# Rebuilding the first periods of a fused attention and feed-forward kernel, and the order of its row minima

## The chip, the cores and the metric

The kernel runs on one core of one Trainium2 chip. The metric is device time in microseconds (us) from launch to the end; lower is better. The engines are TensorE (PE in the profile; its weight loads are PEld), VectorE (DVE), ScalarE (ACT), GpSimd (POOL) and SyncE (SP, which only issues transfers here).

## The reference

Attention with a threshold, followed by a two-layer feed-forward network (called MoE in the names). Shapes: q, k, v are 8 batches x 8 heads x 576 rows x 64; w_in is 512 x 2048, w_out is 2048 x 512; the output is 4608 x 512, all in float32.

```python
scores = scale * np.matmul(q, k.transpose(0, 1, 3, 2))
thresh = np.max(scores, axis=-1, keepdims=True) - tau        # tau = 0.02
scores = np.where(scores >= thresh, scores, -1000000000.0)
scores = scores - np.max(scores, axis=-1, keepdims=True)
attn = np.exp(scores)
attn = attn / (np.sum(attn, axis=-1, keepdims=True) + 1e-09)
x = np.matmul(attn, v)                  # heads side by side: 4608 tokens x 512
h = x @ w_in
g = np.maximum(0.01 * h, h)
out = g @ w_out
```

## The kernel before

**Periods.** The work is cut into 72 periods, nine for each batch: eight periods of 256 query rows of one pair of heads (block 0, pairs 0 to 3; block 1, pairs 0 to 3), and one for the last 64 rows ("tails") of all eight heads. Each turn n of the loop at line 463 emits, in one order written out by hand, the instructions of period n on every engine together with work of other periods. Every engine executes its own instructions strictly in this order, so an instruction that waits holds up all that are behind it on its engine.

In period n:
- PE computes the scores (line 227): four tiles of 128 x 576, for two row blocks c and two heads h, into one PSUM buffer `sc` of five banks. One bank is shared by a piece of head 0 (called a12) and a piece of head 1 (b12). The piece that comes second waits for a signal: an empty instruction (line 246) on POOL, that waits for the last matmul of the first piece. It stands behind POOL's earlier work.
- DVE copies each tile to SBUF with its row minimum (line 257, function `copies`, four instructions), makes the thresholds (`th`, line 259, one small instruction for each period: its start is used below as the mark of a period), then the masked weights of three tiles (line 282, `weights`), and the reciprocals of the row sums (`rec`, line 288, `finish`).
- ACT computes the exponentials: three plain ones (line 271, `exp_plain`), and for the fourth tile a steep Prelu and an exponential with a row sum (lines 276 and 277, `exp_steep`). `rec` needs that row sum.
- In turn n+1 POOL spreads `rec` into the weight tile (line 292, `widen`), and SP issues a transposing transfer wT<-w (line 297, `turn_w`).
- Two turns after its scores (PV_LAG = 2), PE multiplies the transposed weights by v (line 309, `pv`), and DVE scales the result into the token group x (line 329, `evacuate`).
- A group of 256 tokens is complete after four periods. Its layer 1 (line 349, eight units) and layer 2 (line 362, sixteen units) are then queued, and each turn takes two units of layer 1 and four of layer 2 off the queues. This is exactly the rate at which groups arrive. ACT applies the leaky function (line 351) and copies the output (line 368).

**Operands.** q and k of float32 are split into two float16 parts, high and low. On POOL a unit (one pair of heads of q or k) takes three instructions: scale (line 144), cast (150) and subtract (154). The units of the very start are split by ACT (high, line 164) and DVE (low, line 165) in `split_now`. `turn` transposes a unit on PE (line 183) and copies it from PSUM on ACT or DVE (line 190, tails line 186); the k tails are copied once more within SBUF by POOL (line 188). From batch 1 on, units are split and turned ahead of their batch; ten units for each batch, so one or two in a period, none in some.

**Buffers that couple the engines.** The PSUM tag "h" has two buffers; transposes, layer 1 and pv go through them in turn, so the next one waits until ACT or DVE has read the last but one. The score copies and exponentials have one buffer for each tile.

**Start.** q and k of batch 0 are loaded pair by pair, with the k tails on SP behind the first k pair; POOL issues the four w_in loads ahead of the loop (they change float32 to float16 on the way), and the w_out loads in turns 3 to 6. v of batch 0 is cast by POOL in turns 2 and 3.

Of the kernel before, what the change touches and what calls it, by code (L numbers as in the profile page):

```python
# [36 lines left out]
def kernel(  # L37
# [44 lines left out]
    def load_tails(b, which):  # L82
        t = sb.tile([128, 2, 2, 64], FP32, tag="rawt", bufs=2, name="rawt")
        src = SRC[which][b, :, MAIN:S, :].rearrange("(u sh) p d -> u p sh d", u=2)
        for u in range(2):
            nc.sync.dma_start(out=t[ds(64 * u, 64), :, :, :].rearrange("p s h d -> p (s h) d"), in_=src[u])
        tails[b, which] = t
# [35 lines left out]
    turned, halves, scaled = {}, {}, {}  # L123
# [44 lines left out]
    def turn(key, copy=None):  # L168
        copy = copy or nc.scalar.copy
        b, p, which = key  # L170
        dst, half = turned_of(b, which), halves.pop(key)
        n = 2 if p == "t" else 4
        c0 = 0 if which == "q" else 64
        if p == "t":
            c0 = MAIN if which == "q" else 0
# [3 lines left out]
        for x in range(2):  # L179
            for t in range(n):  # L180
                for h in range(2):
                    o = tp[ds(64 * h, 64), x, :, t, :] if p == "t" else tp[ds(64 * h, 64), x, t, :]
                    nc.tensor.transpose(o, half[:, x, t, h, :], ident[:, :])  # L183
        if p == "t":
            for x in range(2):
# [3 lines left out]
        else:  # L189
            copy(out=dst[:, :, p, ds(c0, 512)], in_=tp[:, :, :, :].rearrange("d x t p -> d x (t p)"))  # L190
# [38 lines left out]

    def scores(st):  # L230

        (a00, a01), (b01, b00) = pieces(0, 0), pieces(0, 1)
        (a11, a12), (b12, b11) = pieces(1, 0), pieces(1, 1)
        todo = [[(1, a12), (0, a00), (0, a01), (1, a11)], [(0, b00), (0, b01), (1, b11), (1, b12)]]
        todo = [[(c, x, i) for c, x in row for i in range(3)] for row in todo]
        at_, signal = [0, 0], None
        while todo[0] or todo[1]:
# [3 lines left out]
            for mm in product(st, c, h, x, i):  # L241
                if (h, x) == (1, b12) and i == 0:
                    tc.add_manual_dep(mm.ins, signal.ins.name, BEHIND, reason="the row halves share a bank")
                last = mm
            if (h, x) == (0, a12) and i == 2:
                signal = nc.gpsimd.nop()
                tc.add_manual_dep(signal.ins, last.ins.name, BEHIND, reason="the row halves share a bank")

    TILES = ((0, 1), (0, 0), (1, 0), (1, 1))

    def copies(st):
        st.mn = sb.tile([128, 4], FP32, tag="mn", bufs=2, name="mn")
        st.th = sb.tile([128, 4], FP32, tag="th", bufs=2, name="th")
        st.s = {}
        for n, t in enumerate(TILES):
            st.s[t] = sb.tile([128, 576], FP32, tag=f"s{n}", bufs=1, name="s")
            nc.vector.tensor_scalar(out=st.s[t][:, :], in0=sc[:, ds(PLACE[t], 576)], scalar1=-1.0 / UNIT, scalar2=None,  # L257
                                    op0=AX.mult, op1=AX.min, accum_out=st.mn[:, n : n + 1])
# [3 lines left out]
        st.e = {}  # L262
# [23 lines left out]
    def finish(st):  # L286
# [27 lines left out]
    def evacuate(st, n):  # L314
# [17 lines left out]
        if done:  # L332
            nu = 8 if xg.tokens == 256 else 4
            l1q.extend((xg, u, nu, n + 1) for u in range(nu))
# [62 lines left out]
    def split_at(n, key):  # L397
        if key[0]:
            at(pool_at, n - 2, lambda key=key: split_scale(key))
            at(pool_at, n - 2, lambda key=key: split_high(key))  # L400
            at(low_at, n - 1, lambda key=key: split_low(key))
        else:
            at(pool_at, n - 1, lambda key=key: split_pool(key))
        at(turns_at, n, lambda key=key: turn(key))

    for b in range(1, B):
        base = PERB * (b - 1)
        for i, (s, w_) in enumerate(((0, "k"), (0, "q"), (1, "k"), (1, "q"))):
            at(loads_at, base + ((-2, -1, 2, 3)[i] if b > 1 else (1, 1, 3, 3)[i]),
               lambda b=b, s=s, w_=w_: load_main(b, s, w_))  # L410
        for i, w_ in enumerate("kq"):
# [127 lines left out]
```

## Time and profile before

| | us |
|---|---|
| median of 3 runs | 527.36 (525.57 to 527.87) |
| the profiled execution | 526.85 |
| its span, first to last instruction | 525.1 |
| th of period 0 | 18.87 |
| th of periods 1, 2, 3, 4 | 25.84, 33.41, 43.93, 50.50 |
| th of periods 5, 6, 7, 8, 9 | 57.07, 64.71, 72.22, 82.25, 89.20 |
| th of periods 63 and 71 (the last) | 437.90, 486.15 |

"th" is the start of the threshold instruction of a period in the timeline of the profiled execution. The 1.75 us between the span and the profiled execution's time lie outside the recorded instructions. Busy shares over the span are PE 90%, DVE 83%, ACT 80% and POOL 49%; they mix a start in which engines wait, a middle in which three of them are nearly full, and a last part of layer 1 and layer 2 alone.

### The profile page before, as it was taken

The page shows a single profiled execution, that of the slowest core. Times are in us where ns is not written, and L with a number is a line of the kernel's source. Part 1 is how long each engine was busy: PE and PEld are TensorE (multiplying, and loading weights), DVE is VectorE, ACT ScalarE, POOL GpSimd, SP SyncE. Part 2 cuts the span into 40 slices and gives each one's busy share as a digit, 9 for nine tenths or more (in the row PEclk, how much of TensorE's full clock was granted, in tenths as well). Part 3 has the DMA queues.
Part 4 walks back from the last instruction along what each step waited for, and adds up shares of the span by engine and source line. Part 5 has one row for each costly group of instructions (what it writes and reads, how often), then busy time and mean ns, then how long its engine had stood idle before and what let it go on. Part 6 is the DMA issues. An engine that isn't in the chain of part 4 may idle for free. (4 is left out here: it accounts for less than half of the span.)

```text
span 525.1 us, 18850 instructions
## 1 busy us (share of the span) xinstructions
PE 472.8 (90%) x7744; PEld 372.1 (71%) x7744; DVE 435.1 (83%) x1231; ACT 422.3 (80%) x714; POOL 256.3 (49%) x410
## 2 busy tenths in 40 slices
PE   4666768998989999999999999999999999999995
PEld 3444556776777777777777777777777777777783
DVE  1778868999899999999899989999899989999300
ACT  3567678888989998898989998898989998778541
POOL 5889953655375645654384636563385531100000
PEclk9999689999999999999999999999999999999999
DMA  8978999588988699978998699789988796666511
GB/s 204 241 178 175 201 199 209 112 171 195 205 179 183 123 225 227 173 146 203 215 171 176 170 207 215 160 130 225 201 155 202 158 192 144 122 102 151 133 42 61
DMA packets 230806, 90.34 MB, mean 172 GB/s; under 512 B 201024, under 2 KB 227648, under 8 KB 230720
## 3 DMA queue, kind: packets, MB, share of 16 engines
q1 hardware_dynamic: 227488, 84.43, 76.7%
q0 software_dynamic: 2688, 4.19, 4.7%
q8 instruction: 60, 0.98, 0.8%
q10 hardware_dynamic: 544, 0.52, 0.3%
q14 instruction: 26, 0.21, 0.1%
HBM read 36.70 MB, written 9.44 MB: 88 GB/s over the span
## 5 line engine op out<-in xcount | busy, mean ns | idle before, releaser
L257 DVE TENSOR_SCALAR_CACHE_REDUCE s<-sc 128x576 f32<-128x576 f32 x288 | 199.0, 748 | 12.0 <-PE sc L227 11.5
L282 DVE SCALAR_TENSOR_TENSOR w<-s,th,e 128x576 f16<-128x576 f32 x216 | 184.2, 876 | 8.6 <-ACT e L271 1.1
L271 ACT ACTIVATE e<-s,mn 128x576 f16<-128x576 f32 x216 | 158.7, 773 | 20.2 <-DVE s L257 19.2
L362 PE MATMUL o<-wout,g 128*64 128x512 f16 x1152 | 148.9, 380 | 5.0 <-ACT osb L368 3.5
L349 PEld LDWEIGHTS <-win 128*64 128x64 f16 x2560 | 127.4, 110 | 29.2 <-issue 16.0
L349 PE MATMUL hp<-x,win 128*64 128x256 f16 x2048 | 134.4, 273 | 8.4 <-ACT kT L190 4.5
L227 PE MATMUL sc<-kT,qT 64*128 64x256 f16 (+7 forms) x1920 | 128.4, 298 | 12.0 <-DVE s L257 4.7
L292 POOL CAST w<-rec 128x256 f16<-128x256 f32 x72 | 28.7, 399 | 211.8 <-DVE rec L288 199.6
L227 PEld LDWEIGHTS <-qT 64*128 64x128 f16 (+1 forms) x1920 | 97.9, 101 | 35.0 <-issue 19.5
L351 ACT ACTIVATE g<-hp 128x512 f16<-128x512 f32 x144 | 84.6, 588 | 13.0 <-PE hp L349 13.0
L362 PEld LDWEIGHTS <-g 128*64 128x64 f16 x1152 | 69.6, 110 | 35.5 <-issue 8.5
L154 POOL TENSOR_TENSOR half<-scaled,half 128x512 f16<-128x512 f32 (+1 forms) x77 | 82.5, 1079 | 0.6
L309 PE MATMUL pv<-wT,v 128*64 128x256 f16 (+1 forms) x960 | 55.6, 251 | 12.2 <-DMA wT<-w 6.7
L309 PEld LDWEIGHTS <-v 128*64 128x64 f16 x960 | 44.6, 112 | 25.9 <-POOL v L105 5.3
L277 ACT ACTIVATE w<-s,minus_tau 128x576 f16<-128x576 f32 x72 | 55.8, 775 | 5.8
L276 ACT ACTIVATE s<-s,th 128x576 f32<-128x576 f32 x72 | 55.8, 775 | 0.9 <-DVE th L259 0.9
L183 PE MATMUL tp<-ident,half 128*64 128x128 f16 x1152 | 49.3, 236 | 8.0 <-ACT half L164 5.1
L150 POOL CAST half<-scaled 128x512 f16<-128x512 f32 (+1 forms) x77 | 52.1, 676 | 4.9
L183 PEld LDWEIGHTS <-half 128*64 128x64 f16 x1152 | 38.6, 119 | 22.1 <-issue 15.9
L190 ACT COPY kT<-tp 128x1024 f16<-128x1024 f16 x32 | 32.3, 1010 | 21.4 <-PE tp L183 21.4
L144 POOL TENSOR_SCALAR scaled<-raw 128x512 f32<-128x512 f32 x62 | 40.7, 657 | 10.2 <-DMA raw<-in_q_dram 8.3
L190 ACT COPY qT<-tp 128x1024 f16<-128x1024 f16 x31 | 31.4, 1014 | 14.1 <-PE tp L183 14.0
(32 smaller groups left out, 231.6 us busy)
## 6 DMA issues: line engine op xcount, KB each, us to landing
vraw<-in_v_dram SPq DMA_DIRECT2D x16, 512.0 KB, 5.0
out_dram<-osb SPq DMA_DIRECT2D x16, 512.0 KB, 3.7
raw<-in_k_dram SPq DMA_DIRECT2D x14, 512.0 KB, 4.7
raw<-in_q_dram SPq DMA_DIRECT2D x14, 512.0 KB, 4.4
win<-in_moe_w_in_dram POOLq DMA_DIRECT2D x4, 512.0 KB, 11.5
wout<-in_moe_w_out_dram POOLq DMA_DIRECT2D x4, 512.0 KB, 6.8
wT<-w SPq DMA_TRANSPOSE x72, 5.9
raw<-in_k_dram SPq DMA_DIRECT2D x4, 256.0 KB, 11.0
```

The lines of the kernel that those rows point to most:

```text
L154: nc.gpsimd.tensor_tensor(out=halves[key][:, 1, 0:n, :, :], in0=scaled.pop(key)[:, 0:n, :, :], in1=halves[key][:, 0, 0:n, :, :], op=AX.sub ...
L183: nc.tensor.transpose(o, half[:, x, t, h, :], ident[:, :])
L190: copy(out=dst[:, :, p, ds(c0, 512)], in_=tp[:, :, :, :].rearrange("d x t p -> d x (t p)"))
L227: yield nc.tensor.matmul(out=o, lhsT=lhs, rhs=turned[st.b, "k"][rows, kx, pair, ds(key0, n)], start=(i == 0), stop=(i == 2), skip_group_ch ...
L257: nc.vector.tensor_scalar(out=st.s[t][:, :], in0=sc[:, ds(PLACE[t], 576)], scalar1=-1.0 / UNIT, scalar2=None, op0=AX.mult, op1=AX.min, acc ...
L271: nc.scalar.activation(out=st.e[t][:, :], in_=st.s[t][:, :], func=AF.Exp, bias=st.mn[:, n : n + 1], scale=-1.0)
L276: nc.scalar.activation(out=z, in_=z, func=AF.Prelu, bias=st.th[:, n : n + 1], scale=-1.0, alpha=1e20)
L282: nc.vector.scalar_tensor_tensor(out=w_of(st, t), in0=st.s[t][:, :], scalar=st.th[:, n : n + 1], in1=st.e[t][:, :], op0=AX.is_le, op1=AX.mult,
L309: nc.tensor.matmul(out=o, lhsT=v16[st.b % 2][:, 2 * c + u if st.tail else st.p, blk, :], rhs=rhs, start=(i == 0), stop=(i == 4), skip_grou ...
L349: nc.tensor.matmul(out=hp[ds(64 * c, 64), jj, :], lhsT=w_in16[:, i, ds(128 * j + 64 * c, 64)], rhs=g.x[:, i, :], start=(i == 0), stop=(i = ...
L351: nc.scalar.activation(out=g.g[:, ds(nj * u, nj), :], in_=hp[:, :, :], func=AF.Prelu, bias=0.0, scale=1.0, alpha=0.01)
L362: nc.tensor.matmul(out=g.o[ds(64 * c, 64), :], lhsT=g.g[:, j, ds(128 * m + 64 * c, 64)], rhs=w_out16[:, j, :], start=(j == 0), stop=(j == ...
```

## The change

It does eight things.

1. The two transfers of batch 0's k tails go from SP's queue (behind the first k pair) to ACT's queue (behind the first q pair); k of pair 1 follows at once on SP.
2. The first three units are handled one after the other, each split, transposed and copied before the next: k tails, then k of pair 0, then q of pair 0. The tails are copied by DVE.
3. k and q of pair 1 are split by ACT and DVE (`split_now`), no longer by POOL.
4. The four w_in loads go from ahead of the loop into turns 1 and 2, the w_out loads from turns 3 to 6 into turns 4 to 7. v of batch 0 is cast in turns 1 and 2.
5. The scores are emitted in another order: b12 is now the first piece of head 1 and a12 the last of head 0, so a12 waits for the signal. In periods 0 to 3 the signal is on ACT, later on POOL as before.
6. In every period the row minimum of tile (0, 0) is emitted within the scores, behind the piece that shares its bank, and the matmuls behind it are declared independent of it. `rec` of the period before comes next, then the other three tiles.
7. Where a turn has two units, ACT copies the first, computes the first exponential, and copies the second.
8. In turns 0 to 5, pv and its evacuation stand ahead of MoE and ahead of the weights, and a group that is completed there starts layer 1 in the same turn, that is one turn earlier.

```diff
     def load_tails(b, which, eng=None):
...
-            nc.sync.dma_start(out=t[ds(64 * u, 64), ...], in_=src[u])
+            (eng or nc.sync).dma_start(out=t[ds(64 * u, 64), ...], in_=src[u])
...
-    def turn(key, copy=None):                     # transposes and copies
+    def turn(key):                                # transposes only; keeps tps[key]
+    def take(key, copy=None):                     # the copies out of PSUM
...
+    TILES = ((0, 0), (0, 1), (1, 0), (1, 1))      # was ((0, 1), (0, 0), (1, 0), (1, 1))
     def scores(st):
-        todo = [[(1, a12), (0, a00), (0, a01), (1, a11)], [(0, b00), (0, b01), (1, b11), (1, b12)]]
+        todo = [[(0, a00), (0, a01), (1, a11), (1, a12)], [(1, b12), (1, b11), (0, b01), (0, b00)]]
...
+                if first is not None:
+                    tc.declare_no_dep(mm.ins, first.ins, reason="other banks")
-                if (h, x) == (1, b12) and i == 0:
+                if (h, x) == (0, a12) and i == 0:
                     tc.add_manual_dep(mm.ins, signal.ins.name, BEHIND, reason="the row halves share a bank")
-            if (h, x) == (0, a12) and i == 2:
-                signal = nc.gpsimd.nop()
+            if (h, x) == (1, b12) and i == 2:
+                signal = (nc.scalar if st.n < 4 else nc.gpsimd).nop()
+            if (h, x) == (0, a11) and i == 2:
+                first = copy_min(st, 0)
...
+    def copies(st, before):
+        if before:
+            recip(before)
+        copy_min(st, 1)
+        copy_min(st, 2)
+        copy_min(st, 3)
...
     load_pair(0, "q", nc.scalar)
-    load_tails(0, "k")
+    load_tails(0, "k", nc.scalar)
+    load_pair(1, "k", nc.sync)
     load_pair(1, "q", nc.scalar)
-    load_pair(1, "k", nc.sync)
...
-    for i in range(4):
-        load_w(i)
-        at(pool_at, 3 + i, lambda i=i: load_w(4 + i))
+    first = units(0)
+    for key in (first[2], first[0], first[1]):
+        split_now(key)
+        turn(key)
+        take(key, None if key == first[0] else nc.vector.tensor_copy)
+    for key in first[3:5]:
+        split_now(key)
+    for key in first[5:7]:
+        split_pool(key)
+    for i, key in enumerate(first[3:9]):
+        at(turns_at, i // 2, key)
+    for key in first[7:9]:
+        at(pool_at, 0, lambda key=key: split_pool(key))
+    for i in range(4):
+        at(pool_at, 1 + i // 2, lambda i=i: load_w(i))
+        at(pool_at, 4 + i, lambda i=i: load_w(4 + i))
+    at(pool_at, 1, lambda: cast_vtails(0))
+    for p in range(NP):
+        at(pool_at, 1 + p // 2, lambda p=p: cast_v(0, p))
+    at(pool_at, 2, lambda: split_pool(first[9]))
+    at(turns_at, 3, first[9])
...
     while n < N + PV_LAG or l1q or l2q or stores:
+        early = n < 6
...
-        for f in turns_at.get(n, []):
-            f()
+        keys = turns_at.get(n, [])
+        for key in keys:
+            turn(key)
+        for key in keys[:1]:
+            take(key)
+        if st:
+            exp_plain(st, 0)
+        for key in keys[1:]:
+            take(key)
         for f in pool_at.get(n, []):
             f()
-        if st:
-            exp_plain(st, 0)
+        if early:
+            pv_of(n, n)()
         for half in range(2):
...
-        if n >= PV_LAG and n - PV_LAG < N:
-            pv(periods[n - PV_LAG])
+        x = (lambda: None) if early else pv_of(n, n + 1)
         if st:
             weights(st, 0)
             weights(st, 1)
-        if n >= PV_LAG and n - PV_LAG < N:
-            evacuate(periods[n - PV_LAG], n)
+        x()
         if st:
             weights(st, 2)
-            finish(st)
```

## The prediction

> **What bounds the kernel now.** I read the page first, then the busy times by stretch, the timeline up to period 9, the waits, and the transfers of single stretches. A period is marked by its th (line 259).
>
> ```profile
> span 525.1 us, 18850 instructions
> PE 472.8 (90%) x7744; PEld 372.1 (71%) x7744; DVE 435.1 (83%) x1231; ACT 422.3 (80%) x714; POOL 256.3 (49%) x410
> ```
>
> ```profile
> 18.87:89.20 70.33, 48.99 (x672) 37.40 (x673) 57.11 (x151) 50.70 (x83) 53.00 (x75) 0.90 0.98 197
> 89.20:437.90 348.70, 335.71 (x5747) 266.66 (x5748) 323.43 (x919) 312.01 (x529) 186.91 (x299) 1.00 0.87 179
> 437.90:486.15 48.25, 46.80 (x714) 36.11 (x712) 45.36 (x137) 38.76 (x69) 4.58 (x12) 1.00 0.69 140
> ```
>
> Columns: stretch, length, busy PE, PEld, DVE, ACT, POOL, PE clock, share of the DMA engines, GB/s. The first nine periods take 7.8 us each, the next 54 take 6.46, the last eight 6.03. In the middle PE is busy 96%: there PE leads and DVE follows closely. At the end DVE leads (45.4 of 48.3). In the first stretch no engine is full but the DMA engines are (0.98). From the last th to the end, 39 us, PE works alone at layers 1 and 2; the change leaves that as it is.
>
> So the start holds most of what can be won. DVE needs 57.1 us there plus 0.27 idle for each period (the least in any period), 59.5 together; 10.8 are waits. The timeline shows where:
>
> ```profile
> 15.18 0.82 PE L227 MATMUL sc<-kT,qT 64*128 64x256 f16 x5 [2.31 <-POOLq L246]
> ...
> 18.87 0.60 DVE L259 TENSOR_SCALAR th<-mn 128x4 f32<-128x4 f32 x1
> ...
> 35.28 0.42 PE L309 MATMUL pv<-wT,v 128*64 128x256 f16 x1 [4.35 <-POOL v L105]
> ...
> 38.10 0.42 DVE L329 TENSOR_TENSOR x<-pv,wT 128x256 f16<-128x256 f32 x1 [2.25 <-PE pv L309]
> ...
> 75.51 0.83 PE L309 MATMUL pv<-wT,v 128*64 128x256 f16 x10 [3.36 <-DMA wT<-w]
> ```
>
> Period 0 loses 2.3 us because the signal stands behind POOL's splits; period 3 waits for the casts of v on POOL; period 8 waits for a transposing transfer. Why that one is late, two stretches of the DMA view tell:
>
> ```profile
> q0 software_dynamic: 375, 0.38, 93.0%
> ...
> wT<-w SPq DMA_TRANSPOSE x1, 9.2
> ```
>
> ```profile
> q1 hardware_dynamic: 2855, 0.79, 83.5%
> ...
> wT<-w SPq DMA_TRANSPOSE x1, 5.0
> ```
>
> The first is 48.5 to 51.5 us: only q0, the queue of the weight loads, moves (0.38 MB), none of SP's q1, and the wT issued just before takes 9.2 us. The second is 24 to 29 us without q0: 5.0 us. From 56.5 to 58.5 us q0 moved 0.41 MB and q1 twelve packets. So a weight load of 0.52 MB holds wT up for 2.6 us (at that rate) to 4.1 (at 128 GB/s); the wT of 62.65 took 12.8.
>
> **The change, part by part.** Sums are against the profiled execution, 526.85 us, 0.5 under the median.
>
> *Setup.* k tails now come first, and every unit waits for the one before. The tails are worked on at 6.79 now; in ACT's queue, with no weight loads beside them, I take 5.9 (6.8 at worst). Their two issues, 1.41 on SP now, push ACT's table load (1.28) to 4.5 and q of pair 1 behind them, both ahead of need. From there, by the rows of lines 164, 165, 183, 186, 190: tails split, eight transposes (0.64), two copies: 1.8; k of pair 0: low parts 0.72, transposes 0.6, ACT copy 1.0: 2.4; q likewise 2.5. Scores start at 12.6 instead of 10.38, which costs 2.2. But they no longer meet the signal on POOL: 3.3 us (2.50 + 0.82) bring them to 15.9, the first minimum is done beside them, three of 0.68 and 0.2 follow: th of period 0 at 18.1. **-0.8** (ends -0.8 and +0.1).
>
> *Pair 1 on ACT and DVE* (1.34 and 1.43) lies ahead of 15.2, where DVE needs scores: nothing. If scores came earlier it would cost those 1.4. POOL loses 4.8 us (two units of 2.4).
>
> *Periods 1 and 2.* The signal on ACT stands behind the steep exponentials of the period before; behind the waiting matmul stand the turns and pv on PE. The loop is: signal, five matmuls 0.82, 16 transposes 0.96, take 1.0, exp 0.70, take 1.0, two exps 1.40, steep 1.6: 7.5 us. Now it is 6.96 and 7.58. th comes at 25.6 and 33.1: **-0.3 so far**.
>
> *Period 3.* The loads' issues (0.6 each on POOL) stand ahead of the casts (vtails 0.85, pairs 1.25 each) in turn 1; v's first two pairs are still cast by 28.3, so that wait goes. Next late is wT of period 0: issued at 23.6 with two w_in loads beside it, 23.6 + 5.0 + 2 x 2.6 = 33.8. PE wants it at 32.8. If it is not through when loads 3 and 4 begin (about 33), it lands at 39. I take 34, nearer to the row of 2.6: x at 35.7, three weights 2.6, minima and th: 41.6 instead of 43.93. **-2.3 so far** (a wT at 39: +2.7).
>
> *Period 4.* Two w_in loads (5.2 us) and batch 1's first rows (2.7 us) stand ahead of the next wT: it lands at 44, while PE is ready at 39. x now stands ahead of all three weights, so DVE waits from 41.6 to 45: th at 51.4. **+0.9 so far** (ends -2.5 and +6).
>
> *Periods 5 to 7.* Layer 1 starts in turn 5 behind x, which stands behind th: its Prelu on ACT holds the exponentials behind it. This period costs about 2 us more (first layer-1 period now: 7.64 against 6.57 before it), and the next ones go at 7.1 to 7.6, ACT's sum with two takes. **+1.9 at th of period 7.**
>
> *Periods 8 to 10.* w_out comes one turn later, and layer 1 pauses in turn 9, being a turn ahead. Period 8 then takes 7.6 instead of 10.04, and the pause gives 0.3: **-0.6 in all for the start**. The kernel gains nothing else from the early group, since two units a turn is the rate of arrival.
>
> *From period 10 on.*
>
> ```profile
> DVE rec L288 <- ACT w L277: 11.0, 24, 0.9
> ...
> PE hp L349 <- ACT kT L190: 6.4, 11, 0.7
> ...
> PEld L227 <- POOLq L246: 0.2, 1, 0.2
> ```
>
> (89 to 487 us: waited in total, times, longest.) Putting the first minimum ahead of rec covers DVE's 11.0 us, and 0.13 in every period where rec follows the last weights (39.26 to 39.39): up to 8 us more. But PE has 6.15 us of its own in a period with one turn (scores 1.58, transposes 0.47, layers 3.46, pv 0.64) against DVE's 5.94 to 6.4, so DVE's gain counts only where DVE leads: the last eight periods (0.2 each, 1.6) and about half of the others by 0.05 to 0.1. The second take behind the first exponential ends 1.65 us after the first take, and the second layer-1 unit wants its buffer after 1.73: nothing while the exponential's input is ready, up to 0.7 us in some 12 periods if not. The 6.4 us stay. rec, and so POOL's work, moves back by 0.68. **-3.0** (ends -7 and +4).
>
> Sum: -0.6 - 3.0 = -3.6, that is 523.2 us.
>
> **Rivals.**
>
> *A, more.* The wT transfers are not held up by w_in and the start keeps DVE's pace. For: the DMA engines were idle in 36 to 40 us. Against: 48.5 to 51.5. Starting from 41 at period 3, six periods of 6.7 give th of period 9 at 81, 8 us earlier: 515.8. Chance 0.17. The Trainium skill (DMA: Bandwidth & Descriptors, "Queues, rings and completion order") says that a DMA engine takes turns between the queues it has work for, packet by packet; by that rule the two transfers would advance together and this rival would be nearer. The trace disagrees: twelve packets of q1 against 400 of q0 in 56.5 to 58.5 us.
>
> *B, nothing.* The first minimum still waits for the end of all scores, as it did in period 0 (idle 7.81, though its tile was long done), or PE leads throughout; the middle gives 0: 526.2. Chance 0.20.
>
> *C, slower.* w_in holds up both wT: the first lands at 39, the second at 49, and x ahead of the weights passes both waits of 5 us on to DVE; one of them is half absorbed later. +8.5: 531.7. For: q0 and wT got 115 to 130 GB/s together, and one wT took 12.8 us. Against: two weight loads of 2.6 us fit between turns 1 and 2. It decides when the first wT lands later than 36. Chance 0.16.
>
> *D, slower or even.* POOL's signal. With rec 0.68 later, POOL's splits end later; in the periods where it has 5.3 us of work and 1.1 idle, the signal would stop PE by up to 0.5. Two such periods a batch, 6 us, and the middle's gain gone: 529 (526.2 to 532). Against: the wait is 0.2 us now in the whole middle. Chance 0.08.
>
> **How the numbers follow.** The forecast has 0.39: 523.2, its own range 519 to 527. A difference under 0.5% of the median (2.6 us) cannot be told from none, so faster is below 524.7, slower above 530.0. Faster: 0.30 of the forecast, A, and 0.03 of B: 0.50. Same: 0.09 of the forecast, 0.15 of B, 0.03 of D: 0.27. Slower: C, 0.05 of D, 0.02 of B: 0.23. The range reaches from A to C: 514 to 532.
>
> **What would show it.** Scores of period 0 start near 12.6 with no wait for the signal; th of periods 0, 3, 4, 9 near 18.1, 41.6, 51.4, 88.9; the row of pv waiting for v gone, one of pv or x waiting for wT in turns 2 and 3 in its place; rec no longer waiting for ACT; last eight periods 5.8 each. Wrong: th of period 9 outside 81 to 96, or the middle's 54 periods off 6.46 by over 0.12.

## The result, and the profile after

The changed kernel takes 549.50 us (median of 4 runs, 547.55 to 555.57) against 526.74 us (4 runs) before: a ratio of 1.0452 with a 95% interval of 1.0364 to 1.0540. It is slower by about 23 us, outside the predicted range. Ratios here and below leave out executions over 1.5% longer than the shortest of the same kernel; medians are of all executions. The profiled run took 548.35 us with a span of 546.6, against 526.85 and 525.1 before.

The page of the changed kernel, its first lines:

```profile
span 546.6 us, 18926 instructions
PE 472.4 (86%) x7744; PEld 369.4 (68%) x7744; DVE 447.4 (82%) x1237; ACT 423.4 (77%) x716; POOL 259.1 (47%) x404
```

PE is busy as long as before (472.4 and 472.8 us), so the 21.5 us more in the span are idle time of PE. The busy times by stretch say where (columns as in the prediction; each stretch runs from the same th to the same th as there):

```profile
22.24:111.41 89.17, 48.33 (x678) 37.31 (x678) 56.26 (x152) 51.91 (x84) 47.11 (x71) 0.73 1.02 154
111.41:460.92 349.51, 335.09 (x5734) 264.26 (x5736) 332.61 (x919) 310.96 (x527) 197.37 (x300) 1.00 0.87 181
460.92:507.02 46.10, 46.10 (x719) 35.67 (x716) 44.90 (x137) 39.67 (x70) 4.60 (x12) 1.00 0.73 145
```

The first nine periods take 89.17 instead of 70.33 us, the middle 349.51 instead of 348.70, the last eight periods 46.10 instead of 48.25. With th of period 0 late by 3.4 us (22.24, not 18.87), the start loses 22.2 us, the middle 0.8, the end gains 2.2, and what follows the last th takes 0.6 longer: together 21.5. The granted clock was lower in the start (0.73 against 0.90), but PE's busy time there is not longer (48.33 against 48.99 us), so the clock is not what costs the time.

Within the start one period holds most of it. Period 3, from th to th, first in the kernel before and then in the changed one:

```profile
33.41:43.93 10.52, 6.59 (x52) 4.28 (x53) 6.46 (x17) 4.43 (x9) 10.03 (x18) 1.00 0.57 110
```

```profile
35.62:64.04 28.42, 4.84 (x42) 3.45 (x43) 5.95 (x17) 6.07 (x12) 5.00 (x11) 0.58 1.23 122
```

It lasts 28.42 us, all engines together compute little in it, and the DMA engines are full (1.23; shares of packets that overlap in time add up to over 1). The timeline of the changed kernel names the transfer that all wait for:

```profile
7.46 1.28 ACT L164 ACT_TABLE_LOAD   x1 [7.46 <-DMA rawt<-in_k_dram]
...
16.85 3.06 PE L232 MATMUL sc<-kT,qT 64*128 64x384 f16 x24 [0.79 <-DVE qT L195]
...
22.24 0.67 DVE L275 TENSOR_SCALAR th<-mn 128x4 f32<-128x4 f32 x1
...
27.97 1.32 POOL L114 DMA_DIRECT2D win<-in_moe_w_in_dram  x2
28.06 9.99 SPq L312 DMA_TRANSPOSE wT<-w  x1
...
33.99 1.06 POOL L114 DMA_DIRECT2D win<-in_moe_w_in_dram  x2
...
44.52 18.12 SPq L312 DMA_TRANSPOSE wT<-w  x1
57.28 1.28 PE L324 MATMUL pv<-wT,v 128*64 128x256 f16 x10 [22.11 <-DMA wT<-w]
58.59 0.43 DVE L344 TENSOR_TENSOR x<-pv,wT 128x256 f16<-128x256 f32 x1 [22.43 <-PE pv L324]
61.11 0.62 POOL L144 TENSOR_SCALAR scaled<-raw 128x512 f32<-128x512 f32 x1 [23.04 <-DMA raw<-in_k_dram]
66.36 1.28 PE L324 MATMUL pv<-wT,v 128*64 128x256 f16 x10 [4.25 <-DMA wT<-w]
```

The wT of period 0 is issued at 28.06, beside four loads of w_in, and pv, which needs it, starts at 57.28: 29 us instead of 5. Three engines stop behind it for 22 to 23 us each. PE stands at pv, and the scores of the next period are queued behind pv. DVE stands at x, which in the early group is ahead of the weights. POOL stands at batch 1's raw rows: their issue on SP comes behind the transposing transfer, which held SP for 9.99 us (the next one for 18.12), and once issued, at 38.10, the first of them takes 22.9 us to land (4.2 in the kernel before). The DMA view of the changed kernel from 39 to 54 us shows the two queues at work:

```profile
DMA packets 1029, 1.04 MB, mean 70 GB/s; under 512 B 787, under 2 KB 833, under 8 KB 1029
...
q1 hardware_dynamic: 813, 0.24, 66.1%
q0 software_dynamic: 216, 0.80, 49.6%
```

A share of 100% is 16 engines over these 15 us. A packet of q1 (mostly wT) therefore took on average 0.661 x 16 x 15 / 813 = 195 ns and one of q0 (the weights) 551 ns, and both queues together moved 70 GB/s. Where wT runs without the loads, q1's packets take 23 ns (shown with the experiments).

The waits from th of period 9 to the last th:

```profile
POOL w L307 <- DVE rec L303: 176.0, 58, 5.3
...
PE hp L364 <- ACT kT L195: 7.3, 12, 0.7
```

The row of rec waiting for ACT (11.0 us before) is gone; the row of PE's layer 1 waiting for kT stays, as predicted.

### The profile page after: what moved, and what is told of

Read it like the earlier page. It is cut to its first block, busy times and chain, and to the rows that moved or that the text cites. A ratio compares the mean times of both kernels' runs of the same rounds, so it can differ in the third digit from the quotient of the medians.

```text
span 546.6 us, 18926 instructions
## 1 busy us (share of the span) xinstructions
PE 472.4 (86%) x7744; PEld 369.4 (68%) x7744; DVE 447.4 (82%) x1237; ACT 423.4 (77%) x716; POOL 259.1 (47%) x404
## 4 chain that ended last, share of the span: by engine, by line
PE 57%; ACT 7%; DVE 2%; issue 1%; DMA 1%; POOL 0%; POOLq 0%; DVEq 0%
PE o L377 18%; PE hp L364 16%; PE sc L232 14%; PE pv L324 5%; PE tp L180 4%; ACT kT L195 3%; ACT e L286 1%; DMA wT<-w 1%; ACT osb L383 1%; ACT qT L195 1%; ACT g L366 1%; DVE s L265 1%; DVE w L297 0%; DVE th L275 0%; DVE x L344 0%
## 5 line engine op out<-in xcount | busy, mean ns | idle before, releaser
L265 DVE TENSOR_SCALAR_CACHE_REDUCE s<-sc 128x576 f32<-128x576 f32 x288 | 204.1, 746 | 4.8 <-PE sc L232 1.7
L297 DVE SCALAR_TENSOR_TENSOR w<-s,th,e 128x576 f16<-128x576 f32 x216 | 191.6, 907 | 11.5 <-ACT e L286 4.1
L286 ACT ACTIVATE e<-s,mn 128x576 f16<-128x576 f32 x216 | 159.6, 775 | 15.3 <-DVE s L265 15.1
L364 PEld LDWEIGHTS <-win 128*64 128x64 f16 x2560 | 129.2, 111 | 34.0 <-issue 20.9
L364 PE MATMUL hp<-x,win 128*64 128x256 f16 x2048 | 136.6, 276 | 12.2 <-ACT kT L195 6.7
L232 PE MATMUL sc<-kT,qT 64*128 64x384 f16 (+7 forms) x1920 | 126.3, 293 | 10.4 <-ACT qT L195 3.7
L232 PEld LDWEIGHTS <-qT 64*128 64x128 f16 (+1 forms) x1920 | 94.1, 99 | 35.1 <-issue 14.9
L154 POOL TENSOR_TENSOR half<-scaled,half 128x512 f16<-128x512 f32 (+1 forms) x75 | 79.5, 1069 | 0.4
L180 PE MATMUL tp<-ident,half 128*64 128x128 f16 x1152 | 49.9, 235 | 13.0 <-ACT half L164 10.5
L292 ACT ACTIVATE w<-s,minus_tau 128x576 f16<-128x576 f32 x72 | 55.9, 777 | 6.1 <-POOL half L150 0.4
L150 POOL CAST half<-scaled 128x512 f16<-128x512 f32 (+1 forms) x75 | 55.8, 745 | 8.2 <-PE tp L180 3.6
L144 POOL TENSOR_SCALAR scaled<-raw 128x512 f32<-128x512 f32 x60 | 43.4, 723 | 32.9 <-DMA raw<-in_k_dram 23.0
L291 ACT ACTIVATE s<-s,th 128x576 f32<-128x576 f32 x72 | 55.9, 776 | 0.8 <-DVE th L275 0.8
L344 DVE TENSOR_TENSOR x<-pv,wT 128x256 f16<-128x256 f32 x64 | 26.9, 420 | 34.2 <-PE pv L324 33.8
L195 ACT COPY kT<-tp 128x1024 f16<-128x1024 f16 x32 | 32.3, 1011 | 28.4 <-PE tp L180 28.4
## 6 DMA issues: line engine op xcount, KB each, us to landing
win<-in_moe_w_in_dram POOLq DMA_DIRECT2D x4, 512.0 KB, 16.4
```

The source lines that it names most:

```text
L154: nc.gpsimd.tensor_tensor(out=halves[key][:, 1, 0:n, :, :], in0=scaled.pop(key)[:, 0:n, :, :], in1=halves[key][:, 0, 0:n, :, :], op=AX.sub ...
L232: yield nc.tensor.matmul(out=o, lhsT=lhs, rhs=turned[st.b, "k"][rows, kx, pair, ds(key0, n)], start=(i == 0), stop=(i == 2), skip_group_ch ...
L265: return nc.vector.tensor_scalar(out=st.s[TILES[n]][:, :], in0=sc[:, ds(PLACE[TILES[n]], 576)], scalar1=-1.0 / UNIT, scalar2=None, op0=AX. ...
L286: nc.scalar.activation(out=st.e[t][:, :], in_=st.s[t][:, :], func=AF.Exp, bias=st.mn[:, n : n + 1], scale=-1.0)
L291: nc.scalar.activation(out=z, in_=z, func=AF.Prelu, bias=st.th[:, n : n + 1], scale=-1.0, alpha=1e20)
L292: nc.scalar.activation(out=w_of(st, t), in_=z, func=AF.Exp, bias=minus_tau[:, :], scale=1.0, accum_out=st.sum[:, c, h : h + 1])
```

## The experiments

The first theory is that the loads of w_in, now beside the first transposing transfers, cost the whole loss by themselves. The rivals are the new order of the first units, the early pv and x (they pass a late transfer on to PE and DVE), and the scores' new order with rec behind the first minimum. The kernel before was timed again beside each group of experiments (medians 526.43 to 527.79 us), and a ratio is to those times; so a difference of a microsecond or two between kernels of different groups is not clear of noise. All medians at a glance, with the first two wT, from issue to landing, in each profiled run:

| kernel | median us | ratio to before, 95% | wT of period 0, 1 (us) | th of period 0 / 3 / 9 |
|---|---|---|---|---|
| before | 526.74 | | 5.0, 5.3 | 18.9 / 43.9 / 89.2 |
| changed | 549.50 | 1.0452 (1.0364 to 1.0540) | 29.1, 21.8 | 22.2 / 64.0 / 111.4 |
| e1_win_setup | 524.42 | 0.9973 (0.9935 to 1.0010) | 5.0, 7.8 | 22.4 / 42.0 / 87.5 |
| e2_win_late_only | 538.00 | 1.0211 (1.0144 to 1.0278) | 18.0, 15.0 | 17.4 / 55.9 / 98.3 |
| e3_pv_late | 544.57 | 1.0346 (1.0269 to 1.0423) | 21.8, 20.4 | 22.0 / 56.3 / 106.6 |
| e4_win_turn0 | 525.98 | 1.0018 (0.9981 to 1.0056) | 5.7, 8.5 | 21.9 / 42.3 / 89.3 |
| e5_order | 521.83 | 0.9884 (0.9824 to 0.9945) | 5.0, 8.6 | 18.2 / 37.6 / 84.4 |
| e6_win_pieces | 535.56 | 1.0145 (1.0072 to 1.0219) | 10.1, 16.4 | 22.3 / 44.9 / 98.9 |
| e7_win_one_a_turn | 548.18 | 1.0377 (1.0302 to 1.0453) | 9.2, 10.5 | 23.1 / 44.5 / 112.2 |
| e8_minima_only | 524.39 | 0.9941 (0.9908 to 0.9975) | 5.0, 5.9 | 19.1 / 44.5 / 89.2 |
| e8b_pv_late_best | 521.41 | 0.9904 (0.9867 to 0.9942) | 5.0, 8.5 | 18.2 / 36.9 / 91.9 |
| e9_all_w_setup | 524.95 | 0.9966 (0.9934 to 0.9999) | 14.5, 8.6 | 18.0 / 46.5 / 88.4 |
| e10_plain_act_queue | 529.98 | 1.0127 (1.0062 to 1.0192) | 8.0, 14.3 | 17.9 / 40.4 / 91.0 |
| e11_plain_pool_queue | 528.81 | 1.0068 (1.0037 to 1.0098) | 13.0, 16.1 | 18.0 / 44.2 / 93.4 |
| e12_conv_four | 542.86 | 1.0245 (1.0158 to 1.0333) | 31.4, 17.7 | 18.1 / 63.2 / 113.4 |
| e13_conv_two | 527.10 | 1.0021 (0.9984 to 1.0059) | 12.3, 8.8 | 18.5 / 44.5 / 91.4 |
| e14_plain_two | 528.12 | 1.0024 (0.9990 to 1.0057) | 13.3, 8.4 | 18.1 / 45.0 / 97.0 |

The profiled executions of e8b_pv_late_best and e12_conv_four were each the longest of their kernel (528.81 and 549.08 us).

**e1_win_setup: the changed kernel with the w_in loads back ahead of the loop.**

```
+    for i in range(4):
+        load_w(i)
     first = units(0)
...
-        at(pool_at, 1 + i // 2, lambda i=i: load_w(i))
```

> The changed kernel with the four w_in loads back ahead of the loop, the rest of the change as it is. Theory T (w_in loads running beside the wT transfers of periods 0 and 1 hold them up, and with them PE and DVE): the 17.9 us of period 3 and the 2.9 of period 4 go; w_in now competes with the first k and q rows again, up to 3 us; 526 to 532 us. Rival P (pv and its evacuation ahead of MoE and the weights in turns 0 to 5 is what costs): the loss stays, over 540 us. Rival S (the longer setup, th of period 0 at 22.2 instead of 18.9, is the main loss): 546 us or more, since the setup gets no shorter.

Measured: 524.42 us, 25.1 less than the changed kernel and a little below the 526 to 532 that the first theory expected. wT of period 0 takes 5.0 us again. The nine periods from th to th take 65.14 us, 24 less than in the changed kernel and 5.2 less than before:

```profile
22.39:87.53 65.14, 44.33 (x682) 33.88 (x684) 56.64 (x151) 51.52 (x84) 45.21 (x67) 0.87 0.95 190
```

So where the w_in loads stand decides whether the change loses 23 us or nothing that can be told from noise: the interval of e1_win_setup holds 1.

**e2_win_late_only: the kernel before, with its w_in loads moved into turns 1 and 2 and nothing else.**

```
+    pool_at[1], pool_at[2] = [], []
     for i in range(4):
-        load_w(i)
+        pool_at[1 + i // 2].insert(i % 2, lambda i=i: load_w(i))
```

> The kernel before with only the four w_in loads moved into turns 1 and 2, pv and everything else where it was. Theory T: the wT of period 0 lands near 50 us or later and PE, whose pv stands ahead of the next scores, waits for it; 540 to 548 us. Rival P: pv stands behind the weights here and hides most of the wait; 527 to 531 us. Rival S: the setup is as short as before or shorter; 524 to 528 us.

Measured: 538.00 us, 11.6 more than before in the same group, just under what the first theory expected. The move alone makes the kernel slower; the first wT takes 18.0 us. But it lands at 40.3, and the first pv starts only at 48.15, for another reason:

```profile
44.18 0.61 POOL L144 TENSOR_SCALAR scaled<-raw 128x512 f32<-128x512 f32 x1 [12.81 <-DMA raw<-in_k_dram]
...
47.69 1.43 POOL L105 CAST v<-vraw 128x256 f16<-128x256 f32 x4
48.15 2.25 PE L309 MATMUL pv<-wT,v 128*64 128x256 f16 x10 [17.05 <-POOL v L105]
```

The wait that ends last here is for v, whose casts stand on POOL behind batch 1's raw rows, and the first of these took 11.7 us to land beside the loads (4.2 before). So the loads hold up the raw rows as well as wT. The cost is less than half of the 25 us that the move costs inside the changed kernel; the first two wT were shorter too (18.0 and 15.0 us, not 29.1 and 21.8), and how much of the difference is theirs and how much that of the other edits is not shown.

**e3_pv_late: the changed kernel without the early group, pv and x in all turns where they were before.**

```
-        early = n < 6
+        early = False
```

> The changed kernel with pv and evacuation in the place of before in all turns, w_in in turns 1 and 2 as changed. Theory T: PE still waits for wT ahead of the scores of period 3, so nearly all stays; 543 to 551 us. Rival P: 526 to 532 us.

Measured: 544.57 us, 4.9 less than the changed kernel, with intervals that overlap a little, and within what the first theory expected. By the medians the early pv accounts for about a fifth of the loss; the first wT took 21.8 us here, not 29.1, so part of the 4.9 may be the transfer's own.

**e4_win_turn0: as e1_win_setup, but the loads are issued by POOL behind pair 2's splits, ahead of turn 0.**

```
     for key in first[5:7]:
         split_pool(key)
+    for i in range(4):
+        load_w(i)
...
-        at(pool_at, 1 + i // 2, lambda i=i: load_w(i))
```

> The changed kernel with the four w_in loads in POOL's queue ahead of turn 0, behind the splits of pair 2, where the trace shows the DMA engines idle (14.4 to 28 us). Theory T: w_in is through before the first wT is issued at 28; th of period 3 near 43, period 9 near 89; 524 to 530 us, below e1, since the first rows are not disturbed. Rivals P and S: over 540 us.

Measured: 525.98 us, 1.6 us above e1_win_setup and not below it as expected, with a first wT of 5.7 us. The loads need not lead. The last two of them landed at 28.61 and 31.14, 0.7 and 3.3 us after wT was issued (27.87), and that cost wT 0.7 us.

**e5_order: e1_win_setup with the first units in the old order, all three split before they are turned, k of pair 0 first.**

```
-    for key in (first[2], first[0], first[1]):
+    for key in first[:3]:
         split_now(key)
+    for key in first[:3]:
         turn(key)
-        take(key, None if key == first[0] else nc.vector.tensor_copy)
+        take(key, nc.vector.tensor_copy if key == first[1] else None)
```

> The kernel of e1 (w_in ahead of the loop) with the first three units in the order of before: all three split, then k of pair 0, q of pair 0 and the k tails transposed and copied. Theory T2 (the second loss of the change is its serial setup, in which every unit waits for the k tails and ACT loads its table only behind them; 3.5 us at th of period 0): th of period 0 at 17 to 18.5 instead of 22.4, and the time 3 to 5 us under e1, 519 to 522. Rival: the later periods absorb it, since the transfers set their pace; within 1 us of e1.

Measured: 521.83 us, 2.6 less than e1_win_setup, and 1.2% less than before: the fastest together with e8b_pv_late_best. The intervals of e5_order and e1_win_setup still touch; in the profiled runs th of period 9 comes 3.2 us earlier (84.36, not 87.53). Its timeline against that of the changed kernel:

```profile
3.33 1.28 ACT L164 ACT_TABLE_LOAD   x1 [3.33 <-issue]
...
10.15 3.67 PE L232 MATMUL sc<-kT,qT 64*128 64x384 f16 x24
```

In the changed kernel ACT's table load started at 7.46, when the tails had landed, and scores at 16.85; here the table load is over before the first rows land, and scores start 6.7 us earlier. The first nine periods take 66.20 us from th to th; the rest is as in the changed kernel (349.51 and 46.10):

```profile
18.16:84.36 66.20, 46.90 (x678) 36.41 (x677) 56.67 (x152) 50.52 (x82) 47.22 (x68) 0.80 1.05 202
84.36:433.84 349.48, 334.08 (x5734) 263.42 (x5736) 333.28 (x918) 310.92 (x527) 196.25 (x300) 1.00 0.86 181
433.84:479.94 46.10, 46.10 (x720) 35.68 (x716) 44.90 (x136) 39.63 (x70) 4.61 (x12) 1.00 0.75 145
```

**e6_win_pieces: the changed kernel, each w_in load in four pieces of 512 columns, so that q0's packets are a quarter as large.**

```
-            nc.gpsimd.dma_start(out=w_in16[:, i, :], in_=moe_w_in[ts(i, 128), :])
+            for c in range(4):
+                nc.gpsimd.dma_start(out=w_in16[:, i, ts(c, 512)], in_=moe_w_in[ts(i, 128), ts(c, 512)])
```

> The changed kernel (w_in in turns 1 and 2) with every w_in load cut into four of 512 columns: the same bytes in packets of a quarter of the size. Theory R (the DMA engines take the two queues in turn, packet by packet, so the large packets crowd out the small ones of wT): wT gets four times the share and lands before 45 us; 530 to 540. Theory L (the landing of wT is told only when the weight loads that were started before it are through, and these are slow beside wT whatever their packets): wT of period 0 still lands at 50 us or later; 543 to 552.

Measured: 535.56 us, 13.9 less than the changed kernel with the same bytes in the same turns. The first wT takes 10.1 us, the second 16.4. So the smaller packets, if it is they, halve the loss and no more. The edit also spreads the loads out, since POOL issues sixteen: those of turn 1 go out from 27.82 to 32.3 us and those of turn 2 from 34.98 to 41.9, where the changed kernel's two pairs take 1.3 and 1.1 us. Which of the two helped was not separated.

**e7_win_one_a_turn: the changed kernel with one w_in load in each of turns 1 to 4.**

```
-        at(pool_at, 1 + i // 2, lambda i=i: load_w(i))
+        at(pool_at, 1 + i, lambda i=i: load_w(i))
```

> The changed kernel with one w_in load in each of turns 1 to 4 instead of two in turns 1 and 2. If a load costs a wT some 3 to 4 us each, as the single w_out loads do in the kernel before, every one of four wT is late by that, part of it hidden: th of period 3 near 46, 530 to 536. If any overlap of w_in and wT brings the collapse of 38 to 54 us: 543 to 552.

Measured: 548.18 us, no better than the changed kernel, and not the 530 to 536 of loads that cost a few us each; but the loss has moved. The first three wT take 9.2, 10.5 and 7.6 us with the loads beside them one at a time, and periods 3 and 4 take 8.05 and 10.56 us. Then the last w_in load and the first w_out load meet one wT:

```profile
52.97 7.34 SPq L312 DMA_TRANSPOSE wT<-w  x1
...
54.64 0.84 POOL L117 DMA_DIRECT2D wout<-in_moe_w_out_dram  x1
...
55.48 0.54 POOL L114 DMA_DIRECT2D win<-in_moe_w_in_dram  x1
...
81.31 1.28 PE L324 MATMUL pv<-wT,v 128*64 128x256 f16 x10 [21.05 <-DMA wT<-w]
```

A third load, of w_out, is issued at 63.43. That wT takes 28.2 us and period 6 28.46. Here single loads cost a wT a few us, as the prediction had it, and loads that pile up beside one cost it 23.

**e8_minima_only: the kernel before with the new order of the scores, the first minimum among them and rec behind it, and nothing else; the signal stays on POOL.**

```
-        todo = [[(1, a12), (0, a00), (0, a01), (1, a11)], [(0, b00), (0, b01), (1, b11), (1, b12)]]
+        todo = [[(0, a00), (0, a01), (1, a11), (1, a12)], [(1, b12), (1, b11), (0, b01), (0, b00)]]
...
+            if (h, x) == (0, a11) and i == 2:
+                first = copy_min(st, 0)
...
+    def copies(st, before):
+        if before:
+            recip(before)
```

> The kernel before with only the steady part of the change: the new order of score pieces, the first row minimum within the scores, rec behind it; signal on POOL throughout, start as before. By the prediction's step 3.0 us less than before (7 less to 4 more), with the last eight periods at 5.8 instead of 6.03: 522 to 525. Rival (PE leads in the middle, POOL's signal comes later with rec): 526 to 530.

Measured: 0.9941 of before, that is 3.1 us less. Its stretches from th of period 9 (89.22) on, against 348.70 and 48.25 before:

```profile
89.22:436.96 347.74, 335.19 (x5750) 263.89 (x5752) 332.62 (x918) 311.22 (x528) 197.18 (x300) 1.00 0.89 181
436.96:483.07 46.11, 46.11 (x720) 35.67 (x716) 44.90 (x137) 39.63 (x70) 4.60 (x12) 1.00 0.73 145
```

2.1 us come from the last eight periods, 1.0 from the middle: DVE's 11 us of waits for rec are gone, and where PE leads that wins little.

**e8b_pv_late_best: e5_order with the early group off** (the edit of e3_pv_late).

> The kernel of e5 (w_in ahead of the loop, units in the order of before) with pv and evacuation behind MoE and between the weights in all turns, as before. Theory T3 (pv ahead of the weights in turns 2 to 5 passes each late wT on to DVE, and buys nothing since two units a turn is the rate of arrival): 517 to 520 us. Rival (the group that starts a turn earlier fills PE's idle time): 521 to 525.

Measured: 521.41 us, 0.4 less than e5_order, with intervals that overlap. With the loads out of the way the early pv neither helps nor hurts by more than the noise.

The profiled execution, 528.81 us, shows something else. Its th of period 8 comes at 73.00, 4.8 us ahead of that of e5_order, but period 9 takes 18.9 us, not 6.6, because the seventh wT (64.28) took 21.0 us, with pv waiting 11.35 for it. Beside it stood the last two w_out loads, issued 5.2 us ahead of it and 1.7 behind it. In e5_order, with the same loads at 4.8 ahead and 1.7 behind, this wT took 10.4 us, in e14_plain_two 15.1. So nearly the same arrangement does not have one price. The DMA view of e8b_pv_late_best from 72 to 80 us, where the packets of q0 are of 1 KB:

```profile
DMA packets 1297, 0.48 MB, mean 59 GB/s; under 512 B 1138, under 2 KB 1295, under 8 KB 1295
...
q1 hardware_dynamic: 1135, 0.29, 121.1%
q0 software_dynamic: 160, 0.16, 27.0%
```

The transfers slow down here as in the changed kernel, beside smaller packets and one remaining load.

**e9_all_w_setup: e5_order with the four w_out loads ahead of the loop too.**

```
-    for i in range(4):
+    for i in range(8):
         load_w(i)
...
-        at(pool_at, 4 + i, lambda i=i: load_w(4 + i))
```

> The kernel of e5 with the four w_out loads ahead of the loop too, behind w_in, so that no weight load runs beside a wT from turn 2 on. Theory T (a weight load beside a wT costs 3 to 5 us where that wT has no slack): the long period 6 of e5 (10.9 us) falls to 7.5, and later units of batch 0 and v arrive later by up to 10 us, which takes some of it back; 517 to 523. Rival (the first rows set the pace): the late v stops turns 1 and 2; 524 to 532.

Measured: 524.95 us, 3.1 more than e5_order; the time that the rival expected, though not for its reason, since periods 1 and 2 are no longer than in e5_order. Eight loads are not through when the first wT is issued (24.4); it takes 14.5 us and period 3 takes 16.44. What period 6 wins (8.68 instead of 10.85, no w_out beside its wT) is less. The window ahead of the first wT holds four loads, not eight.

**e10_plain_act_queue: e5_order with four added fp32 loads (half rows of w_in, 0.52 MB each, unconverted, into buffers that nothing reads) on ACT's queue in turns 1 and 2.**

```
+    def load_again(i):
...
+        nc.scalar.dma_start(out=t[:, 0:2, :].rearrange("p a f -> p (a f)"), in_=moe_w_in[ts(i, 128), 0:1024])
...
+    for i in range(4):
+        at(pool_at, 1 + i // 2, lambda i=i: load_again(i))
```

> The kernel of e5 with four added loads, two in each of turns 1 and 2 as the change has w_in: the first half of the rows of w_in, float32 without conversion, 0.52 MB each in rows of 4 KB, on ACT's queue, into buffers that are not used yet. They are not needed; they only run beside wT. Theory X (the collapse needs the converting loads of POOL's queue): a plain load costs its own 1.5 to 2.7 us at most; 522 to 528 us. Theory Y (any large packets on a second queue beside wT do it): 535 to 550.

Measured: 529.98 us, 8.2 more than e5_order, between what the two theories expected.

**e11_plain_pool_queue: the same loads on POOL's queue** (nc.gpsimd in place of nc.scalar).

> The same four added loads on POOL's queue, still without conversion. If the conversion is what slows them: 522 to 528 us, as on ACT's queue. If POOL's queue is: 535 to 550.

Measured: 528.81 us, 7.0 more than e5_order, again between. Which engine issues the loads matters little. But these move half the bytes of the real ones, so conversion and bytes were still mixed up.

**e12_conv_four: e5_order with the four real loads added once more, converting and in whole rows, in turns 1 and 2; e13_conv_two: only the first two of them, both in turn 1; e14_plain_two: the same two rows without the conversion.**

```
+        nc.gpsimd.dma_start(out=t, in_=moe_w_in[ts(i, 128), :])          # t is fp16 in e12 and e13; e14: an fp32 t, out=t.rearrange(...)
...
+    for i in range(4):                                                   # e13, e14: range(2), all in turn 1
+        at(pool_at, 1 + i // 2, lambda i=i: load_again(i))
```

> As e5 (weights loaded ahead of the loop, first units in the old order), with four more converting loads of w_in (1 MB of fp32 each, written as fp16 into buffers that nothing reads yet) issued by POOL in turns 1 and 2, as the changed kernel does with its real ones. The output does not depend on them. If the loads beside the first transposes of the weights are the whole cause, the time rises by 22 to 28 us over e5, to 544 to 550, with the first wT landing about 55 us. If lateness of w_in itself, or something else in the changed kernel, is part of it, the rise is under 15 us.

> As e12 with only the first two of the added loads, both in turn 1. If two converting loads queued at once beside a wT slow both, the first wT lands 8 to 16 us late and the time is 530 to 540. If it takes all four, it stays under 527.

> As e13, the same two rows of w_in (1 MB each) copied as fp32 without conversion. If the conversion is what matters, this costs under half of what e13 does, 522 to 528. If it is the bytes of the source or the rows alone, it costs as much as e13, within 2 us.

Measured: 542.86, 527.10 and 528.12 us: 21.0, 5.3 and 6.3 more than e5_order. For e12_conv_four that is just short of the expected 22 to 28 (the ratio, 1.0245, puts it at 539.8 us), with the first wT landing at 55.4, as expected; e13_conv_two fell short of its 530 to 540; e14_plain_two agrees with e13_conv_two within the 2 us expected. In the DMA view, the first wT from issue to landing in e5_order (with q1's share of 24 to 29 us), e13_conv_two (with the shares of 25 to 37 us), e14_plain_two and e12_conv_four:

```profile
q1 hardware_dynamic: 2802, 0.74, 79.7%
...
wT<-w SPq DMA_TRANSPOSE x1, 5.0
```

```profile
q0 software_dynamic: 288, 1.05, 52.7%
q1 hardware_dynamic: 2655, 0.69, 47.5%
...
wT<-w SPq DMA_TRANSPOSE x1, 12.3
```

```profile
wT<-w SPq DMA_TRANSPOSE x1, 13.3
```

```profile
wT<-w SPq DMA_TRANSPOSE x1, 31.4
```

With two loads the conversion is not it: two converting and two plain loads of the same rows delay wT alike, by 7.3 and 8.3 us, and the times agree within their intervals. Four plain loads of whole rows were not run. The loads are: four of them, in a kernel that needs none of their data, bring back 21 of the 25 us and a first wT of 31 us. That the weights themselves come late falls with it, and so does the order of the first units, which is the old one here. The rest of the change is still in e12_conv_four, and e2_win_late_only shows that without it the same move costs less. The last 4 us are within what single runs of these kernels differ by (535 to 549 in e12_conv_four).

Two loads' cost can be worked out from the shares. In e13_conv_two a packet of q0 took 0.527 x 16 x 12 / 288 = 351 ns; 288 of them on 16 engines are 6.3 us, and with the 5.0 of a wT alone that makes 11.3, near the measured 12.3. For four loads the same sum gives 17.6. It fits e2_win_late_only (18.0); e3_pv_late had 21.8, and the changed kernel and e12_conv_four 29.1 and 31.4: in the changed kernel the packets themselves are slower (551 and 195 ns, above). Why they slow down in some cases and not in others is not settled. The two wT together are longest where 4 MB are read beside them (33 to 51 us; 26.5 in small pieces), and take 21 to 29 where 2 MB are, but e7_win_one_a_turn had 28.2 us beside a piled-up pair, so neither a count of loads nor of bytes is a rule.

## Why the prediction was wrong, by its steps

**Period 3, the term of wT, is the step that failed.** The sum had 23.6 + 5.0 + 2 x 2.6 = 33.8 for its landing, with 39 as the worse end; it landed at 57.1. Of that 4.5 us are a later issue (28.06), the rest is the term per load: 2.6 us was the time of a single load at its full rate, as if the loads beside a wT only stood ahead of it. In the changed kernel the term was 6.0 for each of four loads (29.1 less 5.0, over 4), and the sum had counted two loads at 2.6, its worse end four. Elsewhere it was 2.6 to 5.5 with the loads one at a time (e7_win_one_a_turn), 3.7 to 4.2 each with two (e13_conv_two, e14_plain_two) and 3.3, 4.2 and 6.6 each with four (e2_win_late_only, e3_pv_late, e12_conv_four); the last two w_out loads cost a later wT 2.7 each in e5_order and 8.0 in e8b_pv_late_best. The warning was in the trace of before: the wT of 62.65 that took 12.8 us had two w_out loads beside it, issued at 61.38 and 68.59, which is 3.9 per load. The prediction quoted it and took the smaller row. Four loads were outside all rows of before, and the upper end of 39 left no room for a price of more than 2.6.

**Rival C was the mechanism, and decided as it said** (a first wT later than 36); its price of 8.5 us should have been about 25. It had a chance of 0.16.

**Rival A fell, and so did one reading against it.** The Trainium skill (DMA: Bandwidth & Descriptors, "Queues, rings and completion order") has a DMA engine take turns between its queues packet by packet, and I set twelve packets against 400 in 56.5 to 58.5 us of the trace before as disproof. In the changed kernel both queues do advance side by side: 733 packets of q1 and 260 of q0 from 30 to 37 us, so the trace agrees with turns being taken, as far as such counts can tell. That does not make wT fast. A packet of q0 took 351 ns in e13_conv_two and 551 in the changed kernel, one of q1 23 without loads beside it. Loads cut in four halved the loss (e6_win_pieces), which fits, though the loads were spread out there too.

**Setup: -0.8 forecast, +3.4 measured.** Scores of period 0 started at 16.85, not 12.6. The tails landed at 7.39, where I took 5.9 and 6.8 at worst. I put ACT's table load at 4.5, ahead of need; it waited for the tails (7.46) and pushed the first split to 8.75. From there to the scores the chain took 8.1 us against 6.7 forecast. Putting the old order back made th of period 0 4.2 us earlier and the kernel 2.6 us faster (e5_order). The early signal was right: scores took no wait of POOL's splits.

**Periods 1 and 2** took 13.38 us together, 1.2 less than before, where I had 0.5 more.

**Period 4** ran 9.49 us, forecast 9.8 (51.4 less 41.6), but for a landing at 66.3 instead of 44. **Periods 5 to 7** took 23.75 us, 2.03 more than before: +1.0 was what the forecast had (1.9 less 0.9). **Period 8** took 6.82 instead of 10.03: the wait for the transposing transfer went, as forecast.

**Middle and end: -3.0 forecast, and right for the part alone.** e8_minima_only gives -3.1 (its interval goes from -1.3 to -4.9). In the changed kernel the two stretches give -1.3. The last eight periods run at 5.76 in both (forecast 5.8), and the waits of rec are gone. The middle gave 1.0 in e8_minima_only and cost 0.8 in the changed kernel, and 0.8 in e5_order; its share is not clear, since PE leads there. Rival B falls for the end of the kernel; for the middle it was near. Rival D's row, PE's weight loads waiting for POOL's signal, came to 1.1 us in the whole stretch, not 6.

**Pair 1 on ACT and DVE, and the early pv** were put at nothing. The second is shown (e8b_pv_late_best), as long as wT is in time. When it is late, the early group costs some 5 us more by the medians (e3_pv_late, where wT was also less late); rival C had counted on that. Of the first the changed kernel can't tell: the first minimum (19.43) follows pair 1's low parts on DVE without idle time. In e5_order, where scores started at 10.15 and ended at 13.82, the first minimum had to wait behind pair 1 on DVE until 15.35, as the prediction said of scores that come earlier.

With the edits of the two failed steps taken back (e5_order) the kernel takes 521.83 us, near the 523.2 forecast. That is chance: the sum was made with the loads in the loop and the setup's order changed, and its -0.6 for the start and -3.0 for the rest are -4.8 and -1.4 (up to the last th) in e5_order.

## What to carry to other kernels

Bulk loads that compute does not wait for are best issued where no transfer on the critical path is in flight; count what else is in the DMA engines when a load moves, not only what its own engine has queued. The price of loads beside a critical transfer isn't one figure, neither for each load nor for one arrangement (10.4 to 21.0 us for the seventh wT beside the same two loads): go by the worst row in the trace, and where none has as many queued, leave the upper end wide. Ask too which other transfers stand beside the loads, since in e2_win_late_only the raw rows and not wT were needed last. And a step that reorders the first instructions should be checked for what rides on the first one of an engine, such as its table load.

## What the runs showed of the hardware that I had not expected

- Two queues that share the DMA engines can both collapse: 70 GB/s together from 39 to 54 us, against 149 (e5_order, 24 to 29 us) for one transposing transfer without them, idle slices included. It came with 4 KB packets there and with 1 KB packets in e8b_pv_late_best (59 GB/s from 72 to 80 us). The cause is open.
- With two loads it made no difference for the neighbour whether they convert: 12.3 us beside two converting loads, 13.3 beside two plain ones.
- ACT's table load was placed behind the wait of the first activation in the changed order (7.46) and ahead of it in the old one (1.80 before, 3.33 in e5_order). The first activation's tile is written by two transfers in the one and by one in the other; whether that is the reason wasn't tried.
- Single runs can differ a lot beside such loads: 535.1 to 549.1 us in e12_conv_four, and 518.7 to 528.8 in e8b_pv_late_best, where only later wT have loads beside them; e5_order (520.3 to 522.4) and e7_win_one_a_turn (546.4 to 549.2) varied less.
